# Four interleaved attention layers on one core: loads issued first, clears and filler matmuls put into the plan, normalizers by pairs, last outputs on three engines

## The chip, the cores and the metric

The kernel runs on one core of one Trainium2 chip. A core has a matrix engine (TensorE, PE in the profile; its weight loads are PEld), a vector engine (VectorE, DVE), a scalar engine (ScalarE, ACT), a general engine (GpSimd, POOL) and a queue engine (SyncE, SP) that issues most transfers. Each engine works through its own list of instructions in order and waits on semaphores for the others. The metric is device time in microseconds; the median of the runs is compared. Beside it stands one profiled execution, from which all durations come.

## The reference

The input x has 2048 rows of 512 numbers (bf16). Four layers follow one another, A, B, A, B, each `x = x + layer(layernorm(x))`, with 32 heads of 16 numbers:

```python
def A(x, wqkv, wo):          # sliding window attention
    q, k, v = split_heads(x @ wqkv)
    scores = einsum("bhqd,bhkd->bhqk", q, k) * Dh ** -0.5
    mask = (i - j >= 0) & (i - j < 256)
    p = softmax(where(mask, scores, -1e9))
    return merge_heads(einsum("bhqk,bhkd->bhqd", p, v)) @ wo

def B(x, wqkv, wo):          # linear attention
    q, k, v = split_heads(x @ wqkv)
    phi = lambda t: where(t > 0, t + 1, exp(t)) + 1e-6
    pq, pk = phi(q), phi(k)
    kv = einsum("bhsd,bhse->bhde", pk, v);  z = pk.sum(over s)
    o = einsum("bhqd,bhde->bhqe", pq, kv) / (einsum("bhqd,bhd->bhq", pq, z) + 1e-6)
    return merge_heads(o) @ wo
```

The weights wqkv (512x1536) and wo (512x512) of A and of B are used twice each. The result is bf16.

## The kernel before

**Tiling.** Rows are cut into 16 tiles of 128 (index i) and four chunks of 512 (index I, four tiles u each). The running x stays on chip as f32 in `xres`; the bf16 input is first loaded into the second half of each row of it (`x0`).

**Layer A, chunk by chunk.** `ln_tile` normalizes a tile: statistics on DVE (L427, L428), the inverse root on POOL (L431, L432: an addition and a power), the application on DVE (L439) or POOL (L441, L442), and the transposition into `xnT`, either by matmul with an identity (L406, then a copy L409) or by a transfer from SP (L397). `prep` makes keys, queries and values: `proj` (L387) is four matmuls of 512 columns into one PSUM bank; `k_unit` spreads keys of two heads into `kbd` (L495, L497), `q_unit` copies into `qT` (L374), and `v_unit` copies into `vst` and then sends the values by four transfers from SP (L516) into their places in a block `vbd`, whose other elements must be zero. There are five blocks `vbd` and they are cleared once, on DVE, ahead of everything else (L366). `attention` runs `scores` (L540 products, L558 exponentials from PSUM to `pt` on ACT, L580 and L585 masks on DVE or POOL) and `pv_group` (L611 products of `pt` with `vbd`, whose last row counts the sum, L625 and L626 the division into `o_sb`). `out_A` transposes `o_sb`, multiplies by `woA` and adds to `xres` (L475).

**Layer B.** `b_proj` makes keys, values and queries of a chunk; `phi` is an exponential on ACT (L684), a clip min(e,1)+1e-6 on DVE or POOL (L687), and a maximum on DVE (L690). `kv_unit` (L733, L740) accumulates `kvs` over tiles. When all 16 tiles are in, `kv_final` makes `zb` (sums per head, spread over a head's columns; L754) and `kvn` (L758), and multiplies the latter by `woB` into `wkv` (L768, L374). Then `norm_unit` takes one 128-row block c of `pqT` for one chunk I: one matmul with `zb` (L779), on ACT a logarithm and an exponential of its negative in place (L782, L783, which is 1/den), and on DVE the product back into `pqT` (L786). `p2_tile` multiplies `pqT` of one tile by `wkv`, and `out_rows` adds x. In the last layer the sum goes to a buffer `ost`, of which there are two (L470), and from there to the output (L472). In the third layer (the second A) the normalizers and `p2_tile` of the layer before run chunk by chunk between the chunks of attention.

**What sets the order.** The work inside `fast_network` is handed to a `Planner` as operations with costs per engine, priorities (lower goes first), dependencies, and slots of rings (buffers, PSUM banks). `Planner.run` is a list scheduler that runs when the program is built: it always takes the operation that can start first by its cost table, with ties by priority and then by the order of handing in, on the engine where it would start first (a second number in a cost is a handicap of that engine). It models a half-speed PE after windows with few products (`WIN`, `FULL`). The order in which it takes operations is the order of the instructions on each engine; the waits are then put in by dependency. PSUM has eight banks: scores of three units use 0 to 2, of two units 3 and 4, everything else 5 to 7 (and 4 and 3 while `wide[0]` is true). The start of the program (loads of wA on SP, of four x tiles on ACT's queue, constants, clears) and the end lie outside the plan; the other loads are operations of the plan on SP with release times (L801, L805).

Behind the network stands a second, safe version that runs only if a check on the softmax sums fails; it is not executed here.

## Time and profile before

| What | Value |
|---|---|
| median of 3 runs | 538.38 us (536.83 to 541.53) |
| profiled execution | 539.18 us |
| its span, first to last instruction | 537.5 us |
| mean granted TensorE clock | 0.931 |
| busy PE / DVE / ACT / POOL | 464.3 / 386.7 / 383.8 / 301.0 us |
| read from HBM, written | 6.29 MB, 2.10 MB |
| first layernorm statistics | 12.62 us |
| first key and query products | 20.46 us |
| first product with `vbd` | 38.75 us |
| `zb` of the last layer ready, first normalizer on ACT | 493.73 us |
| first and last addition of the output (L470) | 512.03 and 532.20 us |

Times of instructions are counted from the first instruction. A group of instructions is one line of the program, engine and shape; its row gives the busy time and the mean of one, and after the bar the idle time of the engine in front of them with what ended it. Rows of stages give, for each engine, busy microseconds and the number of instructions, then the granted clock, the share of the transfer engines and GB/s. The chain of waits follows the last instruction back through whatever released each step.

### The profile page before, as it was taken

How to read it: one execution, taken by the hardware profiler on the slowest of the kernel's cores; microseconds unless marked ns; L12 is line 12 of the kernel's file. 1: busy time of each engine (PE TensorE's matmuls, PEld its weight loads, DVE VectorE, ACT ScalarE, POOL GpSimd, SP SyncE). 2: the span in 40 equal slices, each digit the busy share in tenths (PEclk: the TensorE clock that was granted, in tenths of full speed). 3: DMA queues.
4: the chain of work that ended last, by engine and by line, in shares of the span. 5: the costliest groups of instructions: out<-in, count | busy, mean ns of one | idle time of the engine just before them, and what ended most of it. 6: DMA issues, size and time to landing. Idle time of an engine off the chain costs nothing.

```text
span 537.5 us, 14479 instructions
## 1 busy us (share of the span) xinstructions
PE 464.3 (86%) x5634; PEld 228.1 (42%) x5634; DVE 386.7 (72%) x902; ACT 383.8 (71%) x432; POOL 301.0 (56%) x885
## 2 busy tenths in 40 slices
PE   0798897999899998878789989899999988787683
PEld 0335444454445445332334544445555444443131
DVE  7888697677467876778967858677767774687663
ACT  0577697789879897257676858888998886736920
POOL 3556576657856975510654748758775785641000
PEclk9999998899989998996899979999999997988588
DMA  6144453213102110000000233111320100000022
GB/s 195 40 105 113 109 88 72 70 37 66 34 1 41 21 22 2 2 0 0 11 19 17 53 52 62 42 23 36 67 42 21 34 19 11 1 2 1 0 82 81
DMA packets 56380, 22.78 MB, mean 42 GB/s; under 512 B 39920, under 2 KB 56304, under 8 KB 56304
## 3 DMA queue, kind: packets, MB, share of 16 engines
q1 hardware_dynamic: 55728, 21.25, 17.5%
q8 instruction: 46, 0.75, 0.6%
q10 hardware_dynamic: 576, 0.52, 0.3%
q14 instruction: 30, 0.25, 0.2%
HBM read 6.29 MB, written 2.10 MB: 16 GB/s over the span
## 4 chain that ended last, share of the span: by engine, by line
PE 50%; POOL 14%; DVE 12%; ACT 10%; DMA 6%; issue 4%; SPq 2%; DVEq 0%; POOLq 0%; ACTq 0%
PE psb L387 28%; PE psb L540 10%; PE psb L611 10%; POOL phi_e L687 5%; POOL pt L585 4%; ACT pt L558 4%; ACT psb L782 3%; ACT psb L783 3%; DMA out_dram<-ost 2%; DVE ln_st L427 2%; POOL xn L442 2%; SPq L516 2%; DVE vbd L366 2%; POOL ln_rs L432 2%; DMA oT<-o_sb 1%
## 5 line engine op out<-in xcount | busy, mean ns | idle before, releaser
L558 ACT ACTIVATE pt<-psb 128x1536 bf16<-128x1536 f32 (+2 forms) x246 | 286.0, 1216 | 49.6 <-PE psb L540 36.6
L585 POOL TENSOR_SCALAR_AFFINE_SELECT pt<-pt 128x192 bf16<-128x192 bf16 (+2 forms) x604 | 173.8, 320 | 105.9 <-ACT pt L558 103.6
L540 PE MATMUL psb<-qT,kbd 32*128 32x320 bf16 (+4 forms) x1440 | 103.0, 260 | 2.9 <-ACT pt L558 2.8
L611 PE MATMUL psb<-vbd,pt 128*128 128x34 bf16 x2880 | 94.0, 179 | 5.7 <-DVE pqT L690 1.4
L611 PEld LDWEIGHTS <-pt 128*128 128x128 bf16 x2880 | 83.0, 97 | 29.6 <-issue 19.3
L540 PEld LDWEIGHTS <-kbd 32*128 32x128 bf16 x1440 | 37.9, 93 | 79.0 <-issue 72.4
L387 PE MATMUL psb<-xnT,wA 128*128 128x512 bf16 x256 | 65.8, 384 | 6.5 <-DVE xn L439 3.0
L387 PE MATMUL psb<-wB,xnT 128*128 128x512 bf16 x256 | 68.7, 401 | 2.2 <-ACT xnT L409 0.7
L580 DVE TENSOR_TENSOR pt<-pt,tri 128x192 bf16<-128x192 bf16 (+4 forms) x206 | 54.9, 294 | 16.2 <-ACT pt L558 15.7
L684 ACT ACTIVATE phi_e<-psb 128x512 bf16<-128x512 f32 x64 | 38.4, 601 | 20.6 <-PE psb L387 10.0
L387 PEld LDWEIGHTS <-xnT 128*128 128x128 bf16 x384 | 33.5, 100 | 44.5 <-issue 14.6
L427 DVE BATCH_NORM_STATS2 ln_st<-xres 128x6 f32<-128x512 f32 (+1 forms) x64 | 43.7, 684 | 2.2 <-DMA xres<-in_A_x_dram 1.9
L497 DVE TENSOR_TENSOR kbd<-psb,eo 128x512 bf16<-128x512 f32 x57 | 36.9, 682 | 11.3 <-PE psb L387 11.2
L431 POOL TENSOR_SCALAR ln_rs<-ln_mv 128x1 f32<-128x1 f32 x64 | 15.4, 241 | 50.3 <-DVE ln_mv L428 47.8
L475 DVE TENSOR_TENSOR xres<-psb,xres 128x512 f32<-128x512 f32 x48 | 32.5, 683 | 14.6 <-PE psb L387 14.2
L432 POOL TENSOR_TENSOR ln_rs<-ln_rs,mhalf 128x1 f32<-128x1 f32 x64 | 36.9, 577 | 5.4 <-POOL ln_rs L431 0.2
L387 PE MATMUL psb<-wkv,pqT 128*128 128x512 bf16 x128 | 34.6, 420 | 4.4 <-DVE ost L470 2.9
L687 POOL TENSOR_SCALAR phi_e<-phi_e 128x512 bf16<-128x512 bf16 x15 | 29.2, 1947 | 13.1 <-ACT phi_e L684 7.5
L387 PE MATMUL psb<-wA,xnT 128*128 128x512 bf16 x128 | 34.6, 401 | 1.8 <-DMA xnT<-xn 1.8
L442 POOL TENSOR_SCALAR xn<-xres,ln_mv,ln_rs 128x512 bf16<-128x512 f32 x41 | 31.9, 777 | 7.7 <-DMA xnT<-xn 3.6
L387 PE MATMUL psb<-woA,oT 128*128 128x512 bf16 x128 | 33.7, 392 | 1.6 <-DVE pqT L690 0.8
L387 PEld LDWEIGHTS <-wA 128*128 128x128 bf16 x256 | 21.2, 98 | 32.6 <-issue 13.5
(79 smaller groups left out, 471.4 us busy)
## 6 DMA issues: line engine op xcount, KB each, us to landing
vbd<-vst SPq DMA_DIRECT2D x128, 34.0 KB, 1.9
out_dram<-ost SPq DMA_DIRECT2D x16, 128.0 KB, 1.7
wA<-in_A_wqkv_dram SPq DMA_DIRECT2D x3, 512.0 KB, 5.8
xres<-in_A_x_dram SPq DMA_DIRECT2D x12, 128.0 KB, 2.7
wB<-in_B_wqkv_dram SPq DMA_DIRECT2D x12, 128.0 KB, 2.8
xnT<-xn SPq DMA_TRANSPOSE x44, 2.4
xres<-in_A_x_dram ACTq DMA_DIRECT2D x4, 128.0 KB, 4.9
woA<-in_A_wo_dram SPq DMA_DIRECT2D x4, 128.0 KB, 2.3
```

The lines of the kernel that those rows point to most:

```text
L387: nc.tensor.matmul(t["t"][:], lhsT=lhs(c), rhs=rhs(c), start=(c == 0), stop=(c == NCT - 1))
L427: nc.vector.bn_stats(t["st"][:], x())
L432: nc.gpsimd.tensor_tensor(t["rs"][:], t["rs"][:], mhalf[:, 0:1], op=ALU.pow)
L442: nc.gpsimd.tensor_scalar(t["xn"][:], x(), t["mv"][:, 2:3], t["rs"][:], op0=ALU.add, op1=ALU.mult)
L497: nc.vector.tensor_tensor(kbd[r][:, t, :, :, :].rearrange("p m k h -> p (m k) h"), ps()[:, hf * 256:(hf + 1) * 256].unsqueeze(2).to_broadc ...
L540: nc.tensor.matmul(A[:, x, at[x]:at[x] + w, :], lhsT=kbd[half(m)][32 * rg:32 * rg + 32, tt, m % 4, :, :], rhs=qT[I % 2][32 * rg:32 * rg + ...
L558: nc.scalar.activation(body[:, x:y, 0:pos[x], :], t["A"][:, x:y, 0:pos[x], :], ACT.Exp, scale=0.25)
L580: nc.vector.tensor_tensor(v, v, mt, op=ALU.mult)
L585: nc.gpsimd.affine_select(out=v, in_=v, compare_op=ALU.is_ge, fill=0.0, base=1 if kind == 0 else -2, pattern=[[0, n], [2 * sg, 64]], chann ...
L611: nc.tensor.matmul(t["O"][:, u, g, :, :], lhsT=PT[:, s0:s0 + 2, :], rhs=vbd[half(m)][:, m % 4, :, grp[g], :], start=(n == 0), stop=(n == l ...
L684: nc.scalar.activation(t["e"][:], ps()[:], ACT.Exp)
L687: (nc.vector if e == "DVE" else nc.gpsimd).tensor_scalar(t["e"][:], t["e"][:], 1.0, 1e-6, op0=ALU.min, op1=ALU.add)
```

## The change

- **Loads.** All loads are issued at the start, whole matrices instead of quarters: x tiles 0 to 3 first, alternating between SP and ACT's queue, then wA (keys on SP, queries on ACT's queue, values on SP), and on SP x 4 to 7, woA, x 8 to 15, wB in three parts, woB. In the plan they are replaced by release times of their buffers (a made-up engine `HBM`), and SP is held busy for 8 us from 2.0.
- **Clears of `vbd`.** They become five operations of the plan, on POOL or DVE (1.9 each, DVE with a handicap of 2.0), priority 1 + k, released at 5.0 + 2k.
- **Fills.** Where the plan leaves PE idle for more than 0.45 us ahead of an operation (after the first 40), `fill` issues matmuls of 512 columns with the identity on part of wA into a bank that is free by the plan, as many as fit at 0.22 us (0.43 when slow).
- **Normalizers.** `norm_unit` takes two blocks at a time into two adjoining banks (3 and 4, 6 and 7, or 1 and 2): two matmuls, one logarithm and one exponential of 1024 columns, one product on DVE.
- **Last outputs.** The buffers are the four `xn` ones instead of two of their own. For tiles with i % 3 == 1 ACT copies the product into a part of `o_sb` and POOL adds x; the others stay on DVE. The last `p2_tile` have priority 1.9, ahead of the normalizers' 2.
- **Clip of phi** only on DVE.
- **Order.** `out_A` has priority 1.6 always (3 before, except in the last chunk); the first product with `vbd` of a group waits in the plan for the readers of `o_sb`; `oT` has four buffers instead of three; a few costs and the delay of transfers (1.3 to 1.5) are set anew. The constant `bd` is made at once; it stood before the plan's instructions already.

```diff
-    LAT = {"PE": .2, "ACT": .12, "DVE": .12, "POOL": .15, "SP": 1.3}
-    WIN, FULL = 3.413, 3150
+    LAT = {"PE": .2, "ACT": .12, "DVE": .12, "POOL": .15, "SP": 1.5, "HBM": 0.0}
+    WIN, FULL, GAP = 3.413, 3150, .45
...
+            fill = (0, 0)
             if e == "PE":
+                gap = start - free["PE"]
+                if gap > self.GAP and n > 40:
+                    b = [k for k, t in enumerate(self.banks.tiles) if t is not None and not t.left and t.end + .1 <= free["PE"]]
+                    m = int((gap - .1) / (.22 if is_warm(start) else .43))
+                    if b and m:
+                        fill = (b[0], m)
+                        k = int((start - gap / 2) / self.WIN)
+                        mac[k] = mac.get(k, 0) + 512 * m
...
+            self.fill(*fill)
             o.fn(e)
...
-    for j in (1, 0, 2):
-        nc.sync.dma_start(wA[:, :, j * D:(j + 1) * D], A_wqkv[:, j * D:(j + 1) * D].rearrange("(c p) n -> p c n", p=P))
+    wcols = lambda w, j: w[:, j * D:(j + 1) * D].rearrange("(c p) n -> p c n", p=P)
     for i in range(4):
-        nc.scalar.dma_start(x0(i), x_dram[i])
+        (nc.sync if i % 2 == 0 else nc.scalar).dma_start(x0(i), x_dram[i])
+    nc.sync.dma_start(wA[:, :, D:2 * D], wcols(A_wqkv, 1))
+    nc.scalar.dma_start(wA[:, :, 0:D], wcols(A_wqkv, 0))
+    nc.sync.dma_start(wA[:, :, 2 * D:3 * D], wcols(A_wqkv, 2))
+    for i in range(4, 8):
+        nc.sync.dma_start(x0(i), x_dram[i])
+    nc.sync.dma_start(woA[:], wcols(A_wo, 0))
+    for i in range(8, NT):
+        nc.sync.dma_start(x0(i), x_dram[i])
+    nc.sync.dma_start(wB[:, :, D:2 * D], wcols(B_wqkv, 1))
+    nc.sync.dma_start(wB[:, :, 2 * D:3 * D], wcols(B_wqkv, 2))
+    nc.sync.dma_start(wB[:, :, 0:D], wcols(B_wqkv, 0))
+    nc.sync.dma_start(woB[:], wcols(B_wo, 0))
...
-        rings = {"ps": Banks(8), "xnT": Ring(3), "xn": Ring(4), "oT": Ring(3), "ost": Ring(2),
+        rings = {"ps": Banks(8), "xnT": Ring(3), "xn": Ring(4), "oT": Ring(4), 
...
+        pl.banks = rings["ps"]
+        def fill(k, n):
+            for _ in range(n):
+                nc.tensor.matmul(psb[:, k, :], lhsT=identb[:], rhs=wA[:, 0, D:2 * D], start=True, stop=True)
+        pl.fill = fill
...
-        for k in range(NH):
-            nc.vector.memset(vbd[k][:], 0.0)
...
+        for k in range(NH):
+            pl.op({"POOL": 1.9, "DVE": (1.9, 2.0)},
+                  lambda e, k=k: (nc.vector if e == "DVE" else nc.gpsimd).memset(vbd[k][:], 0.0),
+                  1 + k, writes=[B("v", k, 0), B("v", k, 1)], after=5.0 + 2 * k)
...
-            ap = pl.op({"DVE": .45} if first else {"POOL": 1.1, "DVE": (.6, 0.0 if fast else .8)}, f_ap, prio, reads=[B("x", i)],
+            ap = pl.op({"DVE": .45} if first else {"POOL": 1.2, "DVE": (.6, 0.0 if fast else .8)}, f_ap, prio, reads=[B("x", i)],
...
-                ost = slot("ost")
-                def fe(e):
-                    t["o"] = work.tile([P, D], BF, name="ost", tag=f"ost{ost.k}", bufs=1)
-                    nc.vector.tensor_tensor(t["o"][:], ps()[:], xres[:, i, :], op=ALU.add)
-                r = pl.op({"DVE": .69}, fe, EV, reads=[B("x", i)], deps=[o], use=[s], take=[ost])
+                ost = slot("xn")
+                def alloc():
+                    t["o"] = work.tile([P, D], BF, name="ost", tag=f"xn{ost.k}", bufs=1)
+                if i % 3 == 1:
+                    k = i // 3 % 2
+                    sc = o_sb[:, 2 * k:2 * k + 2, :].bitcast(F32)
+                    def fc(e):
+                        nc.scalar.copy(sc, ps().rearrange("p (a b) -> p a b", a=2))
+                    r = pl.op({"ACT": .6}, fc, EV, deps=[o] + [d for gi in range(len(GROUPS)) for d in B("o", gi).r], use=[s], writes=[B("osc", k)])
+                    def fe(e):
+                        alloc()
+                        nc.gpsimd.tensor_tensor(t["o"][:].rearrange("p (a b) -> p a b", a=2), sc, xres[:, i, :].rearrange("p (a b) -> p a b", a=2), op=ALU.add)
+                    r = pl.op({"POOL": 1.0}, fe, prio, reads=[B("x", i), B("osc", k)], take=[ost])
+                else:
+                    def fe(e):
+                        alloc()
+                        nc.vector.tensor_tensor(t["o"][:], ps(), xres[:, i, :], op=ALU.add)
+                    r = pl.op({"DVE": .69}, fe, EV, reads=[B("x", i)], deps=[o], use=[s], take=[ost])
...
-                o = pl.op({"PE": .026 * nmm}, f, prio, reads=reads, deps=list(deps) + ([last] if last else []),
+                o = pl.op({"PE": .026 * nmm}, f, prio, reads=reads, deps=list(deps) + ([last] if last else B("o", gi).r + B("o", gi).w),
...
-                (nc.vector if e == "DVE" else nc.gpsimd).tensor_scalar(t["e"][:], t["e"][:], 1.0, 1e-6, op0=ALU.min, op1=ALU.add)
-            y = pl.op({"DVE": .32, "POOL": (.8, .3)}, f2, EV, deps=[x], use=[es])
+                nc.vector.tensor_scalar(t["e"][:], t["e"][:], 1.0, 1e-6, op0=ALU.min, op1=ALU.add)
+            y = pl.op({"DVE": .32}, f2, EV, deps=[x], use=[es])
...
-        def norm_unit(I, c, prio):
-
-            s = bank()
+        def norm_unit(I, j, prio):
+
+            s = bank(2)
+            s.places = (3, 6, 1)
             t = {}
-            cols = pqT[:, c, I * 512:(I + 1) * 512]
+            cols = pqT[:, 2 * j:2 * j + 2, I * 512:(I + 1) * 512]
             def f(e):
-                t["p"] = psb[:, s.k, :]
-                nc.tensor.matmul(t["p"][:], lhsT=zb[:, c, :], rhs=cols, start=True, stop=True)
-            o = pl.op({"PE": .22}, f, prio, reads=[B("zb", c // 2), B("pq", I, c)], take=[s], kind="den")
+                t["p"] = psb[:, s.k:s.k + 2, :]
+                for n in range(2):
+                    nc.tensor.matmul(t["p"][:, n, :], lhsT=zb[:, 2 * j + n, :], rhs=cols[:, n, :], start=True, stop=True)
+            o = pl.op({"PE": .43}, f, prio, reads=[B("zb", j)] + [B("pq", I, 2 * j + n) for n in range(2)], take=[s], kind="den")
...
-            r = pl.op({"ACT": 1.25}, f_r, prio, deps=[o], use=[s])
+            r = pl.op({"ACT": 2.1}, f_r, prio, deps=[o], use=[s])
...
-        for j, t in ((1, 6.0), (0, 7.5), (2, 9.0)):
-            pl.op({"SP": .01}, lambda e: None, 0, writes=[B("wA", j)], after=t)
...
-        for i in range(4, NT):
-            pl.op({"SP": .6}, lambda e, i=i: nc.sync.dma_start(x0(i), x_dram[i]), 5, writes=[b_x[i]],
-                  after=(6.0, 24.0, 44.0)[i // 4 - 1] + .7 * (i % 4))
...
+        landed = [(b_x[i], 3.5 + .4 * i) for i in range(4)] + [(b_x[i], 11 + .4 * (i - 4)) for i in range(4, NT)]
+        landed += [(B("wA", 1), 7.0), (B("wA", 0), 8.0), (B("wA", 2), 10.5), (B("woA"), 13), (B("wB"), 22), (B("woB"), 24)]
+        for b, t in landed:
+            pl.op({"HBM": .01}, lambda e: None, 0, writes=[b], after=t)
+        pl.op({"SP": 8.0}, lambda e: None, 0, after=2.0)
...
-                out_A(I, a, 1.6 if lastI else 3, by_pe=lastI, actb=0.0 if lastI else ACTB)
+                out_A(I, a, 1.6, by_pe=lastI, actb=0.0 if lastI else ACTB)
...
         for I in range(NI):
-            for c in range(NCT):
-                norm_unit(I, c, 2)
+            for j in range(2):
+                norm_unit(I, j, 2)
         for i in range(NT):
-            p2_tile(i, 2, final=True)
-        late_consts()
+            p2_tile(i, 1.9, final=True)
```

More of the change, by code (lines that the diff above doesn't have):

```diff
@@ L834, in fast_network @@
                     wide[0] = True
[L835 to L836 removed]
+                    for j in range(2):
+                        norm_unit(I, j, 1.5)
                     wide[0] = I < 2
```

34 lines of the change are left out of this document (11 added, 23 removed).

## The prediction

> **What bounds the kernel now.** I read the page first: busy time, the main transfers, the queue landings.
>
> ```profile
> span 537.5 us, 14479 instructions
> PE 464.3 (86%) x5634; PEld 228.1 (42%) x5634; DVE 386.7 (72%) x902; ACT 383.8 (71%) x432; POOL 301.0 (56%) x885
> HBM read 6.29 MB, written 2.10 MB: 16 GB/s over the span
> vbd<-vst SPq DMA_DIRECT2D x128, 34.0 KB, 1.9
> ...
> xres<-in_A_x_dram ACTq DMA_DIRECT2D x4, 128.0 KB, 4.9
> ```
>
> TensorE (PE) is busy 464.3 of 537.5 us, so it sits idle for 73.2. Two further views say where: the busy time by stage, and the granted clock of the core.
>
> ```profile
> 0.00:20.00 20.00, 4.02 (x23) 2.32 (x24) 16.75 (x34) 3.60 (x6) 9.44 (x36) 1.00 0.42 131
> 20.00:80.00 60.00, 56.28 (x715) 27.08 (x714) 46.96 (x107) 46.62 (x49) 35.51 (x117) 1.00 0.45 102
> ...
> 493.20:514.70 21.50, 15.64 (x38) 4.56 (x39) 15.27 (x27) 19.52 (x34) 0.00 (x0) 0.52 0.02 8
> 514.70:537.50 22.80, 11.97 (x52) 4.86 (x50) 9.14 (x14) 0.00 (x0) 0.00 (x0) 0.94 0.27 89
> core 0: 537.5 us, clock 0.931
> ```
>
> The first 20 us hold 16.0 us of PE idleness, the two last stages 5.9 + 10.8 = 16.7, and the 473 us between them 40.5. The clock of 0.931 means that at most 0.069 x 537.5 = 37 us of full clock were withheld; 0.48 x 21.5 + 0.06 x 22.8 = 11.7 of that fall in the two last stages, some 25 in the middle. So the middle is a PE-bound kernel with small holes, and the two ends are not PE-bound at all. What holds the ends is in the chain of waits:
>
> ```profile
> 1.70 1.87 DVE vbd L366
> ...
> 10.82 1.87 DVE vbd L366
> ...
> 12.71 0.61 DVE ln_st L427
> ...
> 493.73 0.67 ACT psb L782
> ...
> 509.05 0.70 DVE pqT L786
> ...
> 514.12 2.48 DMA out_dram<-ost
> ...
> 532.20 0.69 DVE ost L470
> ```
>
> At the head VectorE (DVE) clears the five value blocks until 12.7 before the first layernorm may start. At the tail 16 normalizer units run one after another on ScalarE (ACT) from 493.7 to about 514, and only then are the 16 output tiles written, 514 to 532.9, each pair of them behind the output transfer of the pair before (two buffers).
>
> **The change: the head.** Rows of the timeline, the groups (shapes apart), the chain, and the transfer rate in one early microsecond:
>
> ```profile
> 4.87 0.34 POOL L309 TENSOR_SCALAR_AFFINE_SELECT bd<-bd 128x128 f32<-128x128 f32 x1
> 20.46 3.70 PE L387 MATMUL psb<-xnT,wA 128*128 128x512 bf16 x15
> L368 POOL MEMSET pt<- 128x256 bf16 x5 | 1.6, 311 | 0.0
> L369 POOL MEMSET pt<- 128x192 bf16 x5 | 1.3, 258 | 0.0
> L431 POOL TENSOR_SCALAR ln_rs<-ln_mv 128x1 f32<-128x1 f32 x64 | 15.4, 241 | 50.3 <-DVE ln_mv L428 47.8
> L432 POOL TENSOR_TENSOR ln_rs<-ln_rs,mhalf 128x1 f32<-128x1 f32 x64 | 36.9, 577 | 5.4 <-POOL ln_rs L431 0.2
> L439 DVE TENSOR_SCALAR xn<-xres,ln_mv,ln_rs 128x512 bf16<-128x512 bf16 x16 | 6.5, 413 | 0.8 <-POOL ln_rs L432 0.8
> 477.32 0.41 PE psb L406 x4
> 477.75 0.59 ACT xnT L409
> 7.00:8.00 1.00, 0.00 (x0) 0.00 (x0) 1.00 (x1) 0.00 (x0) 0.00 (x0) 1.00 1.09 344
> ```
>
> In company of the weights the first four x tiles (0.5 MB) took 4.9 us to land; now they lead both queues, so I put them near 4 us and the 1.5 MB of wA near 4 + 1.5/0.344 = 8.4. DVE is free then. The next bound is GpSimd (POOL): its constants end at 5.2, each layernorm asks it for 0.24 + 0.58 = 0.82, and the plan now offers it the clears of vbd. From the two memset rows one costs (0.311 - 0.258)/64 a column, so 0.10 + 2176 x 0.00083 = 1.9 us. By priorities (1 + k against 2) and release times (5.0 + 2k) I expect two clears behind the first layernorm: 5.2 + 0.82 + 3.8 + 3 x 0.82 = 12.3, and with the last xn, its transpose and its copy (0.41 + 0.41 + 0.59, some 1.5 with the hand-overs) the key and query products start near 13.8 instead of 20.46: **6.6 us**. With no clear ahead it would be 10.4; with all five ahead, 0.9. I take 6.6, as the listed release times give two.
>
> Loads pass in front of everything else on SP. All 6.29 MB land near 8.4 + 4.3/0.344 = 21 us, and a value block or a transpose that SP issues at 13 waits until then instead of 1.9 us. What covers it is below among the rivals. In return 20 to 80 loses the loads that stood between value blocks on SP; PE's idle time there is 60 - 56.3 = 3.7, so that is worth 0 to 3.7, and I take **1.5**.
>
> **The middle.**
>
> ```profile
> L687 POOL TENSOR_SCALAR phi_e<-phi_e 128x512 bf16<-128x512 bf16 x15 | 29.2, 1947 | 13.1 <-ACT phi_e L684 7.5 <-DVE kvs L740 4.9
> L687 DVE TENSOR_SCALAR phi_e<-phi_e 128x512 bf16<-128x512 bf16 x49 | 15.5, 316 | 8.9 <-ACT phi_e L684 8.4
> L687 DVE TENSOR_SCALAR phi_e<-phi_e x49: 260/294/512, 108.5 to 493.1; 128x512 bf16<-128x512 bf16 x49
> PE psb L779 <- DVE zb L754: 4.9, 2, 2.5
> PE psb L733 <- DVE pks L690: 2.7, 2, 1.8
> 40.39 0.87 PE psb L387 x4
> 148.59 1.87 PE psb L387 x4
> ```
>
> Fifteen clips of phi go from POOL to DVE, 15 x (1.947 - 0.316) = 24.5 us of latency at most. PE's own waits on what follows them are 4.9 + 2.7 = 7.6; with DVE's and ACT's behind them I take **8**. It adds 4.7 us to DVE, which is 72% busy.
> A DVE clip took 260 to 512 ns, so something already stops some of them. The Trainium skill ("SBUF — State Buffer", section "Who interferes with whom") says that a DVE tensor_scalar in a two-port mode and a GpSimd instruction lock each other out for a whole instruction, which speaks against moving clips to DVE. By that rule the spread is such a lock, and the 15 moved clips would cost 15 x (0.512 - 0.294) = 3.3 us more on DVE; no term here hangs on it.
>
> Clock and fills: four projection matmuls cost 0.87 at full clock (0.22 each) and 1.87 at half. Fills keep PE busy through planned gaps, and stalls that vanish take their slow stretch along; of the 25 us withheld in the middle I take **3** (0 to 12). Normalizers of the third layer by pairs save ACT 8 x 0.4 = 3 (next part), on the path **1**. Against this stand the new waits, for which I have no row: pairs hold two PSUM banks, output transposes come earlier (1.6 for 3), the first product with the values of a group waits for the readers of o_sb, DVE has more to do. I charge **-4** (0 to -20, half of the 40.5 us of middle idleness once more). The sum of the middle with SP's 1.5 is 9.5.
>
> **The tail.**
>
> ```profile
> L782 ACT ACTIVATE psb<-psb,eps 128x512 f32<-128x512 f32 x32 | 21.2, 663 | 9.1 <-PE psb L779 9.1
> L783 ACT ACTIVATE psb<-psb 128x512 f32<-128x512 f32 x32 | 18.6, 582 | 1.0
> L786 DVE TENSOR_TENSOR pqT<-pqT,psb 128x512 bf16<-128x512 bf16 x32 | 21.8, 683 | 9.7 <-ACT psb L783 9.5
> L558 ACT ACTIVATE pt<-psb 128x1024 bf16<-128x1024 f32 x98 | 100.9, 1030 | 2.8 <-PE psb L540 2.5
> ```
>
> A pair costs ACT 1.03 + 1.03 + 0.08 (the logarithm's surplus over the exponential) = 2.1 instead of 2 x 1.245 = 2.5. Eight pairs, 16.8, with two wkv evictions and four output copies (0.58 each, as the exponential of one bank) make 20.3: from 493.7 to 514.0, and the last multiplication (two of 0.683, some 1.3) to 515.3. That is no earlier than before. The gain is that outputs now have the higher priority (1.9 against 2): twelve of the 16 tiles depend on earlier chunks and run on PE during the normalizers. PE needs 20 x 0.22 (normalizers and wkv) + 12 x 0.87 = 14.8 of those 21.6 us, DVE 8 x 1.3 + 10 x 0.69 = 17.3; both fit. Behind the last normalizer stand four tiles, 3.5 on PE, and an addition of 0.7: 519.5, against 532.9. The **13.4** follow in full, as what stands after the last addition is the same. The sum by POOL for one tile in three has no row; between its clears of 0.26 and its clip of 1.95 I take 1, and with four buffers it is hidden. If the products stay at half clock (0.52 granted before) PE needs 20 x 0.44 + 12 x 1.87 = 31 us and the gain falls to about 4; with no copies on the path it is 15.7.
>
> Sum: 6.6 + 9.5 + 13.4 = 29.5, a span of 508.0. The profiled execution took 539.18, 1.7 above its span, and the median shown is 538.38, 0.8 below that execution: 508.0 + 1.7 - 0.8 = **509**.
>
> **The rivals.**
>
> *The load backlog gives the head back.* From 13 to 21 us blocks and transposes on SP queue behind loads, and PE takes its work in order.
>
> ```profile
> xres<-in_A_x_dram SPq DMA_DIRECT2D x4, 128.0 KB, 5.8
> 38.75 0.48 PE L611 MATMUL psb<-vbd,pt 128*128 128x34 bf16 x13
> ```
>
> For it speaks that x tiles issued behind three weight loads took 5.8 us to land. Against it, the first product with values ran at 38.75; 6.6 earlier is 32, 11 us after the backlog. Price: up to the 6.6 and the 1.5, 517.
> The Trainium skill ("DMA: Bandwidth & Descriptors", section "Queues, rings and completion order") says that each engine consumes descriptors in ring order, so that the loads on SP would all go first. By that rule the wait of the early blocks is certain, and the trace's 5.8 agrees; whether PE notices stays as priced.
>
> *The new order eats the middle.* The new waits cost what the clips give, or up to 10 more: 517 to 527. For it: the whole plan is made anew, and 40.5 us of holes in the old one stand against planned ones. Against it: PE was 91% busy in the middle, and each edit there removes work or latency.
>
> *The tail is not interleaved.* If normalizers take the banks first, they end near 513 (no copies between), and the 16 tiles follow at PE's 0.87 each: 513 + 13.9 + 0.7 = 527.6; the tail gives 5.3, so 517. Against it: the given priorities.
>
> *Slower: the fills land on the path.* A fill stands in PE's order before an operation that the plan expected late. Where the real hole is elsewhere, the fill is pure PE time. If the plan sees as many holes as the trace (40.5 + 16.7 = 57 us, some 260 matmuls of 0.22) and all are misplaced, it costs 57: 509 + 57 = 566. It decides from 29.5/57, so from 52% misplaced on; at half clock, from 26%. Against it: the large holes, at the layer ends and in the normalizers, are the same in any plan.
>
> **How the numbers follow.** Forecast 0.60, new order 0.18, backlog 0.09, tail not interleaved 0.07, fills on the path 0.06. The range takes the forecast's own spread (head 0.9 to 10.4, clock up to 12): 499, and reaches to 526 for most of the rivals. About 1% is what a measurement of this kernel can tell from no change. All cases but the last lie below 533; of the new order and the fills I leave 0.05 for within 1% and 0.05 for slower; faster 0.90.
>
> **What would show it.** Right: the first key product before 15 us; no POOL row of the clip at L687; output additions beginning near 500, between normalizers, and the last some 4 us behind the last multiplication; granted clock above 0.96. Wrong: PE waits ended by vbd or xnT transfers between 13 and 30; PE busy time well up with no shorter span (fills); clips that fall late on DVE; new waits on o_sb or on banks in the middle.

## The result, and the profile after

| What | Before | Changed kernel |
|---|---|---|
| median of 4 runs each | 537.61 us (531.07 to 541.53) | **515.88 us** (514.07 to 516.78) |
| ratio of the times | | **0.9631**, 95% interval 0.9539 to 0.9723 |
| profiled execution, its span | 539.18, 537.5 us | 515.63, 513.8 us |
| granted clock | 0.931 | 0.989 |

The change makes the kernel 3.7% faster. One run each of clip_pool (527.93), head_both (529.82, where the median of the other three is 502.19) and before_fills (534.01) further down was in a slow state, which the medians include and the ratios leave out.

The page of the changed kernel:

```profile
span 513.8 us, 14702 instructions
PE 466.8 (91%) x5724; PEld 239.0 (47%) x5802; DVE 379.8 (74%) x896; ACT 386.2 (75%) x415; POOL 277.9 (54%) x860
```

Its busy time by stage (length of the stage, then PE, PEld, DVE, ACT and POOL, the granted clock, the transfers' share and GB/s):

```profile
0.00:20.00 20.00, 7.79 (x34) 3.74 (x35) 15.24 (x36) 5.76 (x10) 16.64 (x45) 1.00 0.86 269
20.00:30.00 10.00, 6.96 (x41) 2.28 (x40) 7.88 (x14) 5.67 (x10) 4.85 (x9) 0.90 0.86 185
...
80.00:478.20 398.20, 376.94 (x4899) 197.67 (x4965) 297.34 (x730) 314.94 (x335) 221.67 (x706) 1.00 0.13 26
478.20:502.60 24.40, 22.86 (x104) 10.04 (x105) 17.84 (x24) 18.89 (x21) 3.81 (x3) 1.00 0.16 53
502.60:513.80 11.20, 3.98 (x17) 1.45 (x15) 2.67 (x4) 0.58 (x1) 2.53 (x2) 0.80 0.25 81
```

Its clock:

```profile
core 0: 513.8 us, clock 0.989
```

Its groups of fills and of clips (count, busy us, mean ns of one):

```profile
L351 PE MATMUL psb<-wA,identb 128*128 128x512 bf16 x158 | 42.3, 380 | 0.6 <-issue 0.2
...
L730 DVE TENSOR_SCALAR phi_e<-phi_e 128x512 bf16<-128x512 bf16 x64 | 19.3, 301 | 16.0 <-ACT phi_e L727 14.9
```

PE is busy no less than before (466.8 us against 464.3), but a part of it is now fills (L351, 42.3 us), all 64 clips are on DVE, and the clock is full from 80 us to the last normalizer. The stage from 20 to 30 us, on the other hand, has a hole that was not there before: PE is busy 6.96 of 10 us. The same stage of the kernel before:

```profile
20.00:30.00 10.00, 9.53 (x59) 3.65 (x58) 6.88 (x14) 7.86 (x13) 3.36 (x10) 1.00 0.35 77
```

Two marks divide the span into head, middle and tail: the first product of keys or queries, and the last of the four instructions that make `zb` ("first and last start" in its row), behind which only normalizers and outputs are left. The rows of the kernel before, then of the changed kernel:

```profile
L754 DVE TENSOR_TENSOR zb<-bd,kvs x4: 416/416/418, 238.2 to 494.2; 128x256 bf16<-128x256 f32 x4
```

```profile
L797 DVE TENSOR_TENSOR zb<-bd,kvs x4: 411/414/417, 232.1 to 479.1; 128x256 bf16<-128x256 f32 x4
```

And its first key product in the timeline:

```profile
17.87 3.80 PE L416 MATMUL psb<-xnT,wA 128*128 128x512 bf16 x16 [0.73 <-ACT xnT L438]
```

| Part | Before | After | Gain | Predicted |
|---|---|---|---|---|
| head, to the first key product | 20.46 | 17.87 | 2.6 | 6.6 |
| middle, to the last `zb` | 494.2 - 20.46 = 473.7 | 479.1 - 17.87 = 461.2 | 12.5 | 9.5 |
| tail, to the end of the span | 537.5 - 494.2 = 43.3 | 513.8 - 479.1 = 34.7 | 8.6 | 13.4 |
| sum | | | 23.7 | 29.5 |

Both ends gave less than predicted and the middle more.

**The head.** The timeline of the changed kernel (start, duration, instruction, and in brackets the idle time before it with what ended it):

```profile
9.52 0.38 DVE L468 TENSOR_SCALAR xn<-xres,ln_mv,ln_rs 128x512 bf16<-128x512 bf16 x1
...
10.58 1.91 POOL L397 MEMSET vbd<- 128x2176 bf16 x1
...
10.67 1.97 DVE L468 TENSOR_SCALAR xn<-xres,ln_mv,ln_rs 128x512 bf16<-128x512 bf16 x1
12.46 0.25 POOL L460 TENSOR_SCALAR ln_rs<-ln_mv 128x1 f32<-128x1 f32 x1
...
13.09 3.62 PE L416 MATMUL psb<-wA,xnT 128*128 128x512 bf16 x8
...
19.85 3.94 SPq L426 DMA_TRANSPOSE xnT<-xn  x3
...
25.67 0.41 DVE L468 TENSOR_SCALAR xn<-xres,ln_mv,ln_rs 128x512 bf16<-128x512 bf16 x1 [1.29 <-DMA xnT<-xn]
...
28.39 1.87 PE L416 MATMUL psb<-xnT,wA 128*128 128x512 bf16 x4 [2.86 <-DVE qT L403]
```

The second `xn` takes 0.38 us; the third, beside the POOL clear of 10.58, takes 1.97, and both end together near 12.5 to 12.6. The inverse root of the fourth tile stands on POOL behind the same clear until 12.46. By then PE has two value products in front (eight matmuls in 3.62 us, 0.45 each against 0.22 at full clock), and the fourth transposition and the keys come only after them. Later the transposes that SP issues at 19.85 stand behind the loads. The chain of waits has the price:

```profile
19.85 5.72 DMA xnT<-xn
...
25.67 0.41 DVE xn L468
```

DVE waits for them at an `xn`, queries and keys behind it on DVE wait too, and PE stands 2.86 us until 28.39.

**The tail.** Timeline of the changed kernel:

```profile
487.99 1.01 ACT L828 ACTIVATE psb<-psb 128x1024 f32<-128x1024 f32 x1
...
488.66 5.34 PE L416 MATMUL psb<-wkv,pqT 128*128 128x512 bf16 x24 [0.49 <-DVE ost L513]
...
493.84 1.48 PE L824 MATMUL psb<-pqT,zb 128*128 128x512 bf16 x6
...
494.57 1.10 ACT L827 ACTIVATE psb<-psb,eps 128x1024 f32<-128x1024 f32 x1
```

ACT ended a normalizer at 489.00 and began the next at 494.57, because PE had six output tiles (24 matmuls) in its list ahead of the next `zb` products. In these 5.6 us ACT only copied three output products. DVE waited 4.7 us for output transfers, 2.6 of them behind the last multiplication, which was over at 502.6:

```profile
DVE ost L513 <- DMA out_dram<-ost: 4.7, 4, 1.9
```

The last addition, on POOL, ended at 509.8, 7.2 behind the last multiplication where I had 4.2.

### The profile page after: what moved, and what is told of

The parts are those of the page before. It is cut to its first block, busy times and chain, and to the rows that moved or that the text cites. A ratio compares the mean times of both kernels' runs of the same rounds, so it can differ in the third digit from the quotient of the medians.

```text
span 513.8 us, 14702 instructions
## 1 busy us (share of the span) xinstructions
PE 466.8 (91%) x5724; PEld 239.0 (47%) x5802; DVE 379.8 (74%) x896; ACT 386.2 (75%) x415; POOL 277.9 (54%) x860
## 4 chain that ended last, share of the span: by engine, by line
PE 66%; DVE 10%; DMA 8%; ACT 6%; POOL 5%; issue 4%; SPq 1%; POOLq 0%; DVEq 0%; ACTq 0%
PE psb L416 36%; PE psb L654 12%; PE psb L583 12%; DMA xnT<-xn 4%; PE psb L351 4%; ACT pt L601 2%; POOL pt L628 2%; DVE pqT L831 2%; DMA oT<-o_sb 2%; PE psb L776 1%; DVE ln_st L456 1%; ACT psb L827 1%; POOL xn L471 1%; DVE xres L518 1%; ACT psb L828 1%
## 5 line engine op out<-in xcount | busy, mean ns | idle before, releaser
L583 PE MATMUL psb<-qT,kbd 32*128 32x320 bf16 (+4 forms) x1440 | 98.4, 255 | 2.7 <-ACT pt L601 1.5
L654 PE MATMUL psb<-vbd,pt 128*128 128x34 bf16 x2880 | 92.3, 178 | 1.5 <-POOL pt L628 0.8
L623 DVE TENSOR_TENSOR pt<-pt,tri 128x64 bf16<-128x64 bf16 (+4 forms) x212 | 53.6, 277 | 29.0 <-ACT pt L601 28.1
L416 PE MATMUL psb<-wB,xnT 128*128 128x512 bf16 x237 | 63.3, 383 | 7.5 <-DMA xnT<-xn 5.7
L416 PE MATMUL psb<-xnT,wA 128*128 128x512 bf16 x235 | 62.7, 384 | 6.0 <-DVE qT L403 2.9
L416 PEld LDWEIGHTS <-xnT 128*128 128x128 bf16 x384 | 32.4, 99 | 46.7 <-issue 10.5
L351 PE MATMUL psb<-wA,identb 128*128 128x512 bf16 x158 | 42.3, 380 | 0.6 <-issue 0.2
L416 PEld LDWEIGHTS <-wA 128*128 128x128 bf16 x256 | 21.9, 98 | 31.5 <-issue 11.9
L416 PE MATMUL psb<-woA,oT 128*128 128x512 bf16 x118 | 31.0, 380 | 3.7 <-DMA oT<-o_sb 2.9
L416 PE MATMUL psb<-wkv,pqT 128*128 128x512 bf16 x125 | 29.6, 379 | 3.7 <-DVE ost L513 1.8
L416 PE MATMUL psb<-xnT,wB 128*128 128x512 bf16 x120 | 31.2, 380 | 0.4
```

The costliest lines, as they stand in the source:

```text
L351: nc.tensor.matmul(psb[:, k, :], lhsT=identb[:], rhs=wA[:, 0, D:2 * D], start=True, stop=True)
L416: nc.tensor.matmul(t["t"][:], lhsT=lhs(c), rhs=rhs(c), start=(c == 0), stop=(c == NCT - 1))
L583: nc.tensor.matmul(A[:, x, at[x]:at[x] + w, :], lhsT=kbd[half(m)][32 * rg:32 * rg + 32, tt, m % 4, :, :], rhs=qT[I % 2][32 * rg:32 * rg + ...
L623: nc.vector.tensor_tensor(v, v, mt, op=ALU.mult)
L654: nc.tensor.matmul(t["O"][:, u, g, :, :], lhsT=PT[:, s0:s0 + 2, :], rhs=vbd[half(m)][:, m % 4, :, grp[g], :], start=(n == 0), stop=(n == l ...
```

## Experiments

All are single edits of the changed kernel unless the text says otherwise; medians in us. Runs in one block share their runs of the kernel before; across blocks the ratios to it are compared.

| Kernel | Median | Ratio to the kernel before, 95% interval |
|---|---|---|
| changed kernel | 515.88 | 0.9631 (0.9539 to 0.9723) |
| no_fills | 529.36 | 0.9882 (0.9814 to 0.9949) |
| late_loads | 513.48 | 0.9563 (0.9491 to 0.9635) |
| clears_act | 517.51 | 0.9649 (0.9582 to 0.9716) |
| norms_first | 512.71 | 0.9559 (0.9493 to 0.9625) |
| clip_pool | 522.61 | 0.9744 (0.9710 to 0.9778) |
| bufs8 | 512.45 | 0.9562 (0.9505 to 0.9619) |
| tail_open | 513.19 | 0.9549 (0.9505 to 0.9593) |
| head_both | 503.48 | 0.9358 (0.9288 to 0.9427) |
| rot8 | 512.31 | 0.9516 (0.9452 to 0.9580) |
| best_a | **496.56** | **0.9236** (0.9174 to 0.9298) |
| before_fills | 529.27 | 0.9871 (0.9793 to 0.9949) |
| singles | 518.10 | 0.9681 (0.9639 to 0.9724) |

**Fills left out (no_fills).** Plan and order are the same; only the spare matmuls aren't issued.

```diff
-            self.fill(*fill)
             o.fn(e)
```

> The changed kernel with its plan and its order of instructions untouched, but the filler matmuls (158 of 512 columns) are not issued; they computed nothing that is used. Theory A, the fills keep the clock up: granted clock falls from 0.989 to 0.95 to 0.97, matmuls of the layer ends and of the last normalizers double, and the kernel takes 3 to 8 us more than the 515.9 of the changed kernel. Theory B, the fills only occupy idle time: the clock falls a little, the time stays within 2 us. Theory C, some fills stand on the path: the time falls by 2 us or more.

Measured 529.36: theory A, but beyond its 3 to 8 us. The fills are worth 13.5 us of the 21.7 between the two medians (537.61 - 515.88). Stages of the kernel without fills, the long one first, then three of 4 us behind the first `zb`; then one of those three in the changed kernel:

```profile
80.00:478.20 398.20, 356.64 (x4714) 187.71 (x4770) 288.44 (x706) 309.41 (x325) 221.19 (x701) 0.92 0.13 26
...
236.00:240.00 4.00, 1.80 (x10) 0.72 (x10) 3.39 (x8) 3.74 (x4) 0.00 (x0) 1.00 0.00 0
240.00:244.00 4.00, 2.17 (x7) 0.66 (x6) 3.39 (x4) 3.62 (x5) 0.00 (x0) 0.60 0.00 0
244.00:248.00 4.00, 4.00 (x11) 1.42 (x10) 2.78 (x5) 3.35 (x4) 0.00 (x0) 0.55 0.00 0
```

```profile
244.00:248.00 4.00, 3.95 (x19) 1.82 (x19) 4.00 (x6) 0.08 (x1) 0.00 (x0) 1.00 0.00 0
```

The timeline of the kernel without fills has the holes of these stages:

```profile
239.63 0.59 PE L823 MATMUL psb<-pqT,zb 128*128 128x512 bf16 x2 [1.45 <-DVE pqT L830]
...
241.67 1.01 PE L823 MATMUL psb<-pqT,zb 128*128 128x512 bf16 x2 [1.23 <-DVE pqT L830]
```

PE is busy 1.80 of 4 us from 236 to 240 and 2.17 from 240 to 244, and the clock falls to 0.60 in the second of these stages and to 0.55 in the next. From 244 to 248 PE is busy all the time and does 11 matmuls where the kernel with fills does 19. That is how a gap of a microsecond is paid twice: once as a gap, once by the work behind it.

The marks without fills, the `zb` group and the timeline:

```profile
L796 DVE TENSOR_TENSOR zb<-bd,kvs x4: 412/416/419, 235.0 to 490.5; 128x256 bf16<-128x256 f32 x4
```

```profile
17.36 3.86 PE L415 MATMUL psb<-xnT,wA 128*128 128x512 bf16 x16 [0.94 <-ACT xnT L437]
```

The middle takes 490.5 - 17.36 = 473.1, against 473.7 before the change, and the tail 527.6 - 490.5 = 37.1. So without fills all the other edits together bring the middle 0.6 us.

**Fills alone (before_fills).** The kernel before, with the lines of the change for `gap`, `fill` and `pl.fill` added to its planner as they stand in the diff above, nothing else.

> The kernel before with the planned-gap matmuls alone (same rule, same size). Theory A (fills hold the granted clock up wherever the plan has holes, as the 13.5 us between the changed kernel with and without them say): clock up from 0.931 to 0.97 or more, 522 to 530. Theory B (they pay only in the new plan, whose holes are planned; in the old one they land in the wrong places): 534 to 540, PE busy time up by 15 us or more with no shorter span.

Measured 529.27 and a clock of 0.980: theory A, at the slow end of its range. It lies 7 us below the kernel before by the ratio (0.0129 x 537) and 9 by the medians of its block (538.30 - 529.27); the interval of the ratio reaches up to 0.9949, so the size is uncertain, but fills gain in both plans. Its marks, in a profiled execution of 525.92 us:

```profile
L769 DVE TENSOR_TENSOR zb<-bd,kvs x4: 411/414/414, 232.5 to 479.8; 128x256 bf16<-128x256 f32 x4
```

```profile
21.26 2.96 PE L402 MATMUL psb<-xnT,wA 128*128 128x512 bf16 x11
```

The middle takes 479.8 - 21.26 = 458.5, no more than the 461.2 of the changed kernel. So the fills by themselves can account for all that the middle gained, though this execution lies 3 us below the median.

**Late loads (late_loads).** x 8 to 15, woA, wB and woB become plan operations on SP again.

```diff
-    nc.sync.dma_start(woA[:], wcols(A_wo, 0))
-    for i in range(8, NT):
-        nc.sync.dma_start(x0(i), x_dram[i])
-    nc.sync.dma_start(wB[:, :, D:2 * D], wcols(B_wqkv, 1))
...
+        for i in range(8, NT):
+            pl.op({"SP": .6}, lambda e, i=i: nc.sync.dma_start(x0(i), x_dram[i]), 5, writes=[b_x[i]],
+                  after=(24.0, 44.0)[i // 4 - 2] + .7 * (i % 4))
...
+            load(woA, A_wo, B("woA"), c, 16 + 2 * c)
```

> The changed kernel, but only x tiles 0 to 7 and wA are issued at the start; woA, x 8 to 15, wB and woB are operations of the plan on SP again, in the pieces and with the release times of the kernel before. Theory A, the backlog of loads gave part of the head back: the transposes that SP issues at about 20 us land after 2.5 instead of 5.7 us, the 2.9 us for which TensorE waits at 28 and the slow clock behind it are gone, the sixth division of the first chunk (70.9 us now) comes 3 to 5 us earlier, and the kernel takes 510 to 513. Theory B, the relief of SP between 30 and 68 us is worth as much: early transposes land sooner, but value blocks wait on SP later, and the time stays at 515 to 518.

**Clears away from POOL (clears_act).** One block is cleared on DVE before the plan, the others by ACT as copies of zeros.

```diff
-            pl.op({"POOL": 1.9, "DVE": (1.9, 2.0)},
...
+        nc.vector.memset(vbd[0][:], 0.0)
...
+        nc.scalar.copy(flat(1), zero)
+        for k in range(2, NH):
+            pl.op({"ACT": 2.1}, lambda e, k=k: nc.scalar.copy(flat(k), zero),
+                  5, writes=[B("v", k, 0), B("v", k, 1)], after=9.0 + 3 * (k - 2))
```

> The changed kernel, but no value block is cleared on GpSimd: the first on VectorE before the plan, while it waits for x, the other four by copies of zeros on ScalarE. Theory A, GpSimd's clears stop VectorE's application of the layernorm (1.97 us instead of 0.38) and VectorE's own clear stands before the first: applications take about 0.4 us, the first key product starts at 10.5 to 12 us instead of 17.9, and the kernel takes 510 to 513. Theory B, the backlog of loads sets the pace of the first 30 us anyway: the key products start early as well, but TensorE then waits for transposes that land after 24 us, and the time stays at 514 to 517.

**Both head edits (head_both).** The two diffs above in one kernel.

> The changed kernel with both head edits tried singly: clears on DVE before the plan and on ACT, and the late loads (x 8 to 15, woA, wB, woB) back in the plan. Singly they gave 517.5 and 513.5. Theory A (the lock cost the start, the backlog cost what follows, and each hid the other's gain): first key products near 13.1 and no wait of PE for transposes between 20 and 30, first chunk of attention ends near 64 instead of 70.9, and 509 to 511. Theory B (the head is not kept through the first chunks, whose end is set by the value blocks and exponentials): first chunk ends at 67 or later, 512 to 516.

The stage from 20 to 30 us, of late_loads, of clears_act and of both together:

```profile
20.00:30.00 10.00, 9.76 (x67) 3.51 (x66) 7.71 (x16) 8.83 (x13) 3.99 (x12) 1.00 0.50 125
```

```profile
20.00:30.00 10.00, 5.46 (x28) 1.80 (x28) 4.29 (x9) 4.39 (x6) 2.67 (x9) 0.83 0.55 134
```

```profile
20.00:30.00 10.00, 9.77 (x75) 3.71 (x74) 6.32 (x17) 9.12 (x11) 5.03 (x16) 1.00 0.33 86
```

Two rows of the chain of waits of clears_act (the value part of wA, and the transposes), and the first key product in the timeline of head_both:

```profile
2.22 9.17 DMA wA<-in_A_wqkv_dram
...
19.55 5.19 DMA xnT<-xn
```

```profile
13.35 5.11 PE L413 MATMUL psb<-xnT,wA 128*128 128x512 bf16 x16
```

Late loads alone fill the hole (9.76 of 10 us) but leave the start at 17.9. The first chunk of attention (counted to the start of its last reciprocal on DVE) ends at 67.7 instead of 70.9, as theory A had it, and the median, 513.48, just misses its range. Clears alone bring the start to 13.1, and a longer hole gives it back (5.46 of 10 us): the first chunk ends at 72.4, and the median is no better than that of the changed kernel, theory B. Neither edit alone is told from the changed kernel by the intervals of the ratios. The start at 13.1 is near the 13.8 that I had predicted by accident: 13.8 stood for two clears on POOL, and without any my sum gives 10.0. What held it was wA, whose value part landed at 11.4, where I had put it at 8.4, and a value product ahead of the keys.

With both edits the first chunk ends at 66.1, and the median falls by 12 us, more than theory A's 5 to 7. The theory is right in kind. Why two edits worth about -2 and +2 alone are worth 12 together is shown only in part. At the first `zb` of the second layer both together are 7.0 us ahead of the changed kernel (225.1 against 232.1), while late_loads (233.7) and clears_act (239.8) are behind it: up to there each does need the other. From there to the last `zb` another 10.5 us are gained (461.6 against 479.1), where neither edit issues anything, and late_loads and clears_act are faster in this stretch too (240.7 and 239.2 us against 247.0). So that part comes from a plan that was made anew; no run separates what in it.

**The tail: normalizers first (norms_first).**

```diff
-            p2_tile(i, 1.9, final=True)
+            p2_tile(i, 2, final=True)
```

> The changed kernel with the last output tiles at priority 2 instead of 1.9, so that a normalizer pair that could start at the same time goes first. Theory A, the outputs starve ScalarE, which is the bound of this stretch: its wait of 5.4 us for a normalizer product at 489 to 494.6 is gone, and the last addition comes 3 to 5 us earlier, 511 to 513 in all. Theory B, the output buffers and transfers set the end (VectorE waited 4.7 us for them): normalizers end earlier, the outputs follow at the pace of the buffers, and the time stays within 2 us or grows.

ACT's normalizers now run without a break, and the last multiplication ended at 494.83 instead of 502.6. (The 5.4 us of the expectation stand in a row of waits for the whole kernel. That wait lies in the third layer and is in both kernels; the break in the tail was the 5.6 us shown above.) But the last addition ended at 508.97 instead of 509.8: the wait moved to the buffers, as in theory B. The median, 512.71, lies in theory A's range; the profiled execution (515.45) shows no gain in the tail (513.6 - 477.6 = 36.0 us), and the intervals of the two ratios overlap, so a gain of 3 us isn't shown. What stood ahead of the additions on DVE:

```profile
L513 DVE TENSOR_TENSOR ost<-psb,xres x11: 680/691/692, 488.6 to 508.3; 128x512 bf16<-128x512 f32 x11
...
  DMA out_dram<-ost: 8.0, 8
```

**Eight buffers (bufs8), and an extra bank for outputs (tail_open).** Buffers are the two `qT` tiles in eight parts instead of the four `xn`; tail_open has one line more.

```diff
-                ost = slot("xn")
+                ost = slot("ost")
...
-                    t["o"] = work.tile([P, D], BF, name="ost", tag=f"xn{ost.k}", bufs=1)
+                    t["o"] = qT[ost.k // 4][:, ost.k % 4, :]
...
+                s.places = (0, 5, 7, 4, 3)
```

Both have normalizers first, as above.

> The kernel with the last normalizers ahead of the outputs (512.71), and with eight output buffers (the two qT tiles, idle by then) instead of the four xn ones. There DVE waited 8.0 us and POOL 5.1 us for output transfers, and the last addition ended at 508.97. Theory A (buffers gave the gain of the normalizers back): these waits go, the twelve tiles left at 492.7 follow at 0.95 us each, the last addition ends near 505.5, so 508.5 to 510. Theory B (the transfers themselves set the pace: 16 of 128 KB through one queue, 20 us of issuing): buffers only move the wait, 512 to 514.

> As the one with eight output buffers, and outputs may also use PSUM bank 0, which no normalizer pair uses, so that they run between the normalizers without holding them. Theory A (PE has room: 16 tiles at 0.95 beside eight pairs of 0.6): ACT runs the pairs without a stop, tiles of the first two chunks are written before 494, eight or fewer are left then, and the last addition ends near 500 to 502: 504 to 507. Theory B (the list order and the in-order engines leave the outputs behind the normalizers all the same): as the one with eight buffers alone, 508 to 510.

512.45 and 513.19: neither moved from the 512.71 of norms_first, bufs8 in theory B's range and tail_open above both of its ranges. DVE still waited 6.1 and 5.3 us for transfers. The reason is in the plan: `Ring.free_at` gives out the lowest-numbered buffer that is free, and counts it free once SP has issued its transfer (0.6 us in the plan), not when that has landed. In the changed kernel the 16 outputs use buffer 0 eight times, buffer 1 five times, buffer 2 three times and buffer 3 never. With eight buffers four are used.

**Eight buffers in turn (rot8).** With norms_first, buffers in idle `pt` tiles, and a ring that goes round:

```diff
+class Turn(Ring):
+    n = 0
+    def free_at(self, slot, now):
+        t = self.tiles[self.n]
+        return None if t is not None and t.left else (max(now, 0.0 if t is None else t.end + .1), self.n)
+    def put(self, slot, k):
+        super().put(slot, k)
+        self.n = (k + 1) % len(self.tiles)
```

> The last normalizers ahead of the outputs (512.71), and eight output buffers (pt tiles, idle by then) that are taken in turn. With the eight qT buffers DVE and POOL waited as before (6.1 and 5.1 us), and the plan's list shows why that run told nothing of the buffers: a ring gives out the lowest-numbered buffer that is free by the plan, which counts it free once its transfer has been issued, so only four of the eight were used and buffer 0 seven times in sixteen. Theory A (reuse of the buffer whose transfer has just been issued is what gives the gain back): DVE's and POOL's waits for output transfers go, the last addition ends near 505, and 508 to 510. Theory B (the queue of transfers sets the pace): the waits stay, 512 to 514.

The waits for transfers are gone, and PE's own pace is what is left (what DVE's additions waited for; and PE's timeline):

```profile
L527 DVE TENSOR_TENSOR pt<-psb,xres x11: 683/691/693, 489.8 to 505.2; 128x512 bf16<-128x512 f32 x11
...
  PE psb L428: 3.7, 6
```

```profile
494.63 10.52 PE L428 MATMUL psb<-wkv,pqT 128*128 128x512 bf16 x47 [0.75 <-DVE pt L527]
```

Twelve of the 16 tiles still run at the very end, 10.5 us in one piece. The tail, as above from the last `zb`, is 511.5 - 478.8 = 32.7 us against 34.7. Neither in the median (512.31) nor in the ratio can this be told from norms_first or bufs8: the waits went as theory A said, but the time lies in theory B's range (512 to 514).

**Clips back on POOL (clip_pool).**

```diff
-            y = pl.op({"DVE": .32}, f2, EV, deps=[x], use=[es])
+            y = pl.op({"DVE": .32, "POOL": (.8, .3)}, f2, EV, deps=[x], use=[es])
```

> The changed kernel, with the clip of phi allowed on POOL again as in the kernel before (cost 0.8 with a handicap of 0.3). Theory A (the prediction's term): the clips moved to DVE are worth 8 us of the middle, so 515.9 + 8 = 524 (518 to 532); some 10 to 20 POOL clips of about 1.95 us come back and PE and DVE wait for the pks and pqT behind them. Theory B (the planned gaps and the new order would have hidden them): 515 to 517, with the same number of POOL clips in the trace. Theory C (the planner now puts hardly a clip on POOL): 515 to 517 and fewer than five POOL clips.

```profile
L730 POOL TENSOR_SCALAR phi_e<-phi_e 128x512 bf16<-128x512 bf16 x16 | 31.1, 1941 | 13.7 <-ACT phi_e L727 13.1
L730 DVE TENSOR_SCALAR phi_e<-phi_e 128x512 bf16<-128x512 bf16 x48 | 14.4, 300 | 12.4 <-ACT phi_e L727 11.5
```

Sixteen clips go to POOL, and the median rises by 6.7 (522.61 - 515.88; 6.1 by the ratios). All runs lie above those of the changed kernel (519.97 and more, against 516.78 and less). Theory A; the term was 8.

**Normalizers one by one (singles).** `norm_unit` takes one block and any single bank, as before the change.

```diff
-            s = bank(2)
-            s.places = (3, 6, 1)
+            s = bank()
...
-            r = pl.op({"ACT": 2.1}, f_r, prio, deps=[o], use=[s])
+            r = pl.op({"ACT": 1.25}, f_r, prio, deps=[o], use=[s])
```

> The changed kernel with the normalizers one block at a time again, in any of the banks that other products use, in the third layer and at the end. Theory A (my terms: pairs save ACT 8 x 0.4 in the third layer, 1 of it on the path, and some 3 of the tail, since 16 singles are 16 x 1.245 = 19.9 and 8 pairs 16.8): 518 to 520, 2 to 4 above 515.9. Theory B (pairs hold two banks, and PE waits at each pair for the multiplication that frees them, 2.0 us of each 2.1; singles free a bank sooner and PE gets to the outputs): 511 to 515.

518.10 (516.66 to 521.51), 2.2 above: it points to theory A and speaks against B, though the intervals of the two ratios overlap.

**All of it (best_a).** Both head edits, normalizers first, buffers in turn.

> Late loads and clears on DVE and ACT (503.48 together), with the last normalizers ahead of the outputs and eight output buffers in turn. Theory A (head and tail are apart, gains add): 503.5 less the 3 to 7 us that the tail without transfer waits gives, 496 to 500. Theory B (the tail is set by the rate of the transfers or by the normalizers): 502 to 504.

```profile
80.00:460.00 380.00, 367.30 (x4828) 190.62 (x4885) 300.73 (x740) 307.79 (x323) 224.54 (x704) 1.00 0.15 30
460.00:484.00 24.00, 17.33 (x77) 7.37 (x78) 18.98 (x26) 17.81 (x19) 3.80 (x3) 1.00 0.12 39
484.00:495.00 11.00, 4.42 (x21) 1.80 (x19) 2.79 (x5) 1.17 (x2) 2.54 (x2) 0.90 0.36 115
```

496.56, ratio 0.9236: theory A. It beats the changed kernel by about 4% (0.9236 / 0.9631 = 0.959), and is 7 us below the two head edits alone. On the changed kernel the same tail edits gave 3.6 (515.88 - 512.31): the tail of head_both had grown to 38.9 us (500.5 - 461.6), and that of best_a is 33.7.

## Why the prediction was right, and where it was not

The sign, the forecast case and the order of size were right: 515.88 lies in the range of 499 to 526 and 6.9 above the 509. The sum came closer than its terms, because the ends' misses (4.0 and 4.8 us) were partly made up by the middle (+3.0). That is luck: in the middle one term was far too small and hid others that were too large.

- **Head: 6.6 predicted, 2.6 measured.** The step that failed is "5.2 + 0.82 + 3.8 + 3 x 0.82 = 12.3": I put the clears into POOL's list and asked what they delay there. I left out that an `xn` on DVE and a clear on POOL don't run side by side (1.97 us against 0.38), that DVE itself took one clear at 6.01, in spite of its handicap, and that PE would take value products ahead of the keys. The 8.4 for wA was too early as well (11.4 in clears_act), though it did not decide here. The Trainium skill ("SBUF — State Buffer", section "Who interferes with whom") says that a DVE `tensor_scalar` in a two-port mode and GpSimd shut each other out for a whole instruction; this trace agrees, with DVE ending at 12.64 beside a clear that ends at 12.49. I had weighed that rule for the clips only, where it did not show: the 64 clips average 301 ns, and their term held.
- **The backlog** was a rival at 0.09 ("the load backlog gives the head back"). It was no alternative to the forecast: it happened inside it. I had argued that "the first product with values ran at 38.75", 11 us after the backlog, and looked only at value blocks. What came late were the transposes of the second chunk: DVE's next `xn` stood behind them, and the first chunk's last key and query products on PE, at 28.39, stood behind DVE. The sign I had named, PE waits between 13 and 30 behind such transfers, is in the trace, with DVE between (2.86 us). The last reciprocal of the first chunk then came at 70.9, against 68.6 before: at that point the head and SP's 1.5 were worse than nothing.
- **Fills and clock: 3 predicted (0 to 12), 13.5 measured by removal, 7 to 9 alone.** The failed step is "of the 25 us withheld in the middle I take 3". I took a stall and its slow stretch as one thing that vanishes with the stall, though the fills act where stalls stay. With them the clock between 80 and 478 us is 1.00 instead of 0.92. PE's busy time did rise, by 376.94 - 356.64 = 20.3 us in the same window, but the rival "fills land on the path" is refuted as a net effect by the shorter span.
- **New waits: -4 charged (0 to -20).** Without fills the middle gained 0.6. The clips are worth 6.7 and the pairs about 2 over the whole kernel, though both were measured with fills, so the new order and the early loads together cost some 6 to 8 by difference. Part of that is the loads: late_loads, which moves them back, takes 474.4 - 17.88 = 456.5 in the middle against 461.2, and already by the end of the first chunk the changed kernel had lost its lead. The charge had the right sign; what in the order costs the rest was not tested, and PE's waits give no single culprit.
- **Clips: 8 predicted, 6.7 measured. Pairs: 1 in the third layer and a shorter ACT list in the tail predicted, 2.2 in all measured.** Both hold within what can be told.
- **Tail: 13.4 predicted, 8.6 measured.** That PE needs 14.8 of those 21.6 us held as a sum of work (15.5 without the fills from 479.1 to 502.6), and the order spoilt it: priority 1.9 lets six tiles go ahead of the normalizer that ACT could do next (5.6 us). "with four buffers it is hidden" failed as well, because the ring uses buffer 0 for every second output. Priority alone moved that loss into the buffers (norms_first), and of eight buffers the ring used four (bufs8). With the ring in turn the tail is 2.0 us shorter, since PE then has twelve tiles left; the tails of norms_first and bufs8 (36.0 and 33.7), whose waits are much alike, differ by as much. My POOL addition was too low too: 1.27 us, not 1.

The signs I had named: no POOL clip is left (right), the clock is 0.989 (right), the first key product is not before 15 us (wrong), and additions begin between normalizers, at 487.9 and not near 500, and end 7.2 behind the last multiplication, not 4 (half right).

## What to carry to other kernels

When a step is moved to another engine, look for what it shuts out on the first one, and for the transfers that the moved issues now stand in front of: the start of this kernel had two such costs, and up to the first `zb` only mending both paid. Where a planner leaves PE short holes, spare matmuls there are cheap insurance: price the slower work behind each hole and not only the hole. And read which buffer a ring really gives out before adding buffers to it.

## What was not expected of the hardware

- **Short holes lower the clock.** In the kernel without fills, between 80 and 478 us, the longest stretch without a matmul is 2.18 us, there are 29 of more than 0.45 us, and they add up to 31.5 us; the granted clock there is 0.92, and it was 0.55 and 0.60 in the two stages shown. The Trainium skill ("TensorE: Matmul & The Clock Gate", section "Why this matters for your kernels") advises against idle gaps above some 3 us. By that row alone the fills would have been worth little; the measurement decides: a PE that is half idle from 236 to 244 us, with no gap above 1.5 us, is enough.
- **Transposes behind a backlog** took 5.72 us (changed kernel) and 5.19 (clears_act), against 2.50 for the same transfer in clears_act at 34.13, after the loads had landed, and a median of 2.4 over seven such transfers in late_loads up to 45 us.
- **SP paused between loads.** Timeline of the changed kernel:

```profile
6.10 0.65 SPq L289 DMA_DIRECT2D woA<-in_A_wo_dram  x1
...
9.92 4.89 SPq L291 DMA_DIRECT2D xres<-in_A_x_dram  x8
...
16.43 0.51 SPq L295 DMA_DIRECT2D woB<-in_B_wo_dram  x1
```

Nothing that the trace shows stands between 6.75 and 9.92, and the loads alone keep SP until 16.94. A value block or transpose that is ready earlier can't be issued by SP before that. What held SP for those 3.2 us no run here separates.
